# Moving attention's weighted sums one place along a hand-written interleave

## The chip, the cores and the metric

The kernel runs on one core of a Trainium2 chip. The metric is the device time of one execution in microseconds (us). A core has five engines that run side by side, each through its own queue in order: PE (TensorE, matmuls, with its weight loads shown as PEld), DVE (VectorE), ACT (ScalarE), POOL (GpSimd) and SP (SyncE, which issues most DMAs here). Results of PE land in PSUM, eight banks of 128 x 512 float32 numbers; everything else is computed from and to SBUF.

## The reference

x has 2048 rows (tokens) of 448 numbers. It is normalised, goes through an attention branch and a gated feed-forward branch, and both are added to x:

```python
xn = _layernorm(x, axis=-1)
return x + _A_ref(xn, ...) + _B_ref(xn, ...)
# _A_ref: 16 heads of 28, 4 segments of 512 tokens
for s in range(N):
    qs, ks, vs = q[:, :, s], k[:, :, s], v[:, :, s]
    logits = jnp.einsum("bhqd,bhkd->bhqk", qs, ks) * scale + mask
    p = _softmax(logits, axis=-1)
    a_dot = jnp.einsum("bhqk,bhkd->bhqd", p, vs)
    ...
    o = g * a_mem + (1.0 - g) * a_dot
# _B_ref: h = _sigmoid(xn @ w_gate) * (xn @ w_up);  h @ w_down   (448 -> 1792 -> 448)
```

`a_mem` is a read from a memory that grows from segment to segment. The change touches `a_dot` alone: the softmax's sums over the values, their division by the softmax's own sum, and the factor 1 - g.

## The kernel before, in words

**Stages.** The front part (up to line 577) normalises, makes queries, keys and values, stores them to DRAM, and computes the memory read, which goes to DRAM tensors `od`. Then, from line 785 on, three things are woven together: the feed-forward branch (`gated`, lines 166 to 270), attention within the segments (`attention`, lines 700 to 734), and at the end the output projection (`project`, lines 749 to 779). Each is a generator that stops at every `yield`. Lines 787 to 794 run through the steps of feed-forward and projection and advance attention by so many of its own steps ("places") that it gets done in proportion:

```python
want = min(round(n_att * (k - LEAD) / (N_FFN + N_OUT - LEAD - TAIL)), n_att)
```

Here `n_att` is 16 * 14 + 10 = 234 places, and the divisor is 548 + 61 - 15 - 53 = 541 steps. A feed-forward group of matmuls for gate or up (`pgu`, line 247, eleven matmuls) is followed by three steps, and a group of the down projection (`pd`, line 173, six matmuls) by two.

**Order.** `tc.manual_schedule(engines=MANUAL)` with `MANUAL = {PE, SP}` (line 55): in this stage PE and SP keep the program's order. The order on DVE, ACT and POOL is made when the kernel is built, by a scheduler that takes an instruction when its inputs should be there, the earlier in the program the sooner.

**Attention.** A `Pair` (line 583) is two heads of one segment, a `Unit` (line 670) four heads, so 32 pairs and 16 units. A pair works in ten parts:

- five parts of `scores` (603): one or two matmuls into a bank `st` of two (line 612), ACT copies the bank into the pair's buffer `w` (616, 619), POOL masks (627), DVE takes maxima (629, 633). `w` has three buffers, so pair n + 3 writes where pair n was.
- five parts of `weights` (639): the maxima are merged with POOL's help (643 to 653); DVE spreads them by a transpose to `mb` (656); then three times DVE subtracts (666) and ACT takes the exponential (667).

`Unit.finish` (681) has two parts. The first (687) has 32 small matmuls on PE, the *sums* `pa`, four keys' blocks times four heads times the values `vv`, and one DVE transpose into the buffer of the unit's second pair (690). The second is the division: a reciprocal (135), a product (136), a transpose back (693), and a store to `od` from POOL's queue that adds to what is there from the second segment on (694).

A round of 14 places per unit u goes by a table, where 0 and 1 are a score part of the unit's first and second pair, 2 is the first part of `finish` of unit u - 1, and 3 its second part:

```python
SLOT = (0, 0, 0, None, 0, 0, 2, 3, 1, 1, 1, None, 1, 1)
```

When a pair's five score parts are done, its five parts of `weights` go to a list `behind`, and each place first takes one of them. So the first pair's weights are made at places 6 to 10, and the second pair's at places 0 to 4 of the next round; the sums of a unit come at place 6 of the round after. After them SP is given the load of the next values (`load_values`, 679). Round 16 only finishes unit 15; it has a table of its own with ten places (lines 710 to 715).

Of the kernel before, what the change touches and what calls it, by code (L numbers as in the profile page):

```python
# [35 lines left out]
LEAD, TAIL = 15, 53  # L36


SLOT = (0, 0, 0, None, 0, 0, 2, 3, 1, 1, 1, None, 1, 1)

PARTS = 5

# [19 lines left out]
def kernel(  # L62
# [637 lines left out]
    def attention():  # L700
        for n in range(2):
            pairs[n].load()
        units[0].load_values()
        yield
        run, behind = {}, []
        for u in range(len(units) + 1):
            for n in range(2):
                run[n] = pairs[2 * u + n].scores() if u < len(units) else iter(())
            for k, which in enumerate(SLOT):
                if u == len(units):  # L710

                    if k > 9:
                        break
                    which = (None,) * 8 + (2, 3)
                    which = which[k]
                if behind:
                    next(behind.pop(0))
                if which is not None and which < 2 and u < len(units):
                    next(run[which])
                    n = 2 * u + which + 2  # L720
                    if which not in SLOT[k + 1:]:
                        behind += [run[which]] * PARTS
                        if n < len(pairs):
                            pairs[n].load()
                        else:
                            load_sums(n - len(pairs))
                if which == 2 and u > 0:
                    fin = units[u - 1].finish()
                    next(fin)
                    if u < len(units):  # L730
                        units[u].load_values()
                if which == 3 and u > 0:
                    next(fin)
                yield

    sums = {}
# [1 line left out]
    def load_sums(b):  # L738

        if b < 2:  # L740
            sums[b] = sb.tile([P, HG, L], F32, name="sums", tag="qk2", bufs=2)
        else:
            sums[b] = sums[b - 2]
        o3 = od[b].rearrange("(h c) n -> h c n", c=32)
        for m in range(8):
            a, c = m % 2, 4 * min(m, 6)
            nc.sync.dma_start(sums[b][64 * a:64 * a + 64, m // 2, :], o3[:, c:c + 4, :])
# [32 lines left out]

    N_OUT = 1 + NB * NT * 3 + 12
    steps = attention()
    n_att = len(units) * len(SLOT) + 10
    done = 0
    with tc.manual_schedule(engines=MANUAL):
        next(steps)
        k = sum(FILLS) + 6
# [46 lines left out]
```

## Time and profile before

| what | us |
|---|---|
| median of 3 runs (689.37 to 689.55) | 689.55 |
| the profiled execution, its own time | 689.46 |
| span of its instructions | 687.7 |
| DVE busy in the span | 567.4 |
| ACT busy in the span | 342.6 |
| POOL busy in the span | 151.3 |

The span runs from the first instruction to the end of the last; 1.8 us of the execution lie around it. In the profile's rows, a group has the line, engine, operation, tiles (output <- inputs), shapes and count, then the group's busy time, the mean length of one in ns, and after the second bar the engine's idle time just before them with what ended it. A row of the timeline has start, length, engine, line and operation, tiles and count. A row of waits has the waiting engine and line, who ended the wait, the sum in us, how often, and the longest. A row of windows has the stretch, its length, the busy time (and instructions) of PE, PEld, DVE, ACT and POOL, the granted clock of PE, the DMA engines' share and their GB/s. PE's matmuls overlap in the profile and their ends are modelled, so where PE's time goes is read from starts.

### The profile page before, as it was taken

How to read it: one execution, taken by the hardware profiler on the slowest of the kernel's cores; microseconds unless marked ns; L12 is line 12 of the kernel's file. 1: busy time of each engine (PE TensorE's matmuls, PEld its weight loads, DVE VectorE, ACT ScalarE, POOL GpSimd, SP SyncE). 2: the span in 40 equal slices, each digit the busy share in tenths (PEclk: the TensorE clock that was granted, in tenths of full speed). 3: DMA queues.
4: the chain of work that ended last, by engine and by line, in shares of the span. 5: the costliest groups of instructions: out<-in, count | busy, mean ns of one | idle time of the engine just before them, and what ended most of it. 6: DMA issues, size and time to landing. Idle time of an engine off the chain costs nothing.

```text
span 687.7 us, 10438 instructions
## 1 busy us (share of the span) xinstructions
PE 681.7 (99%) x3594; PEld 566.6 (82%) x3594; DVE 567.4 (83%) x994; ACT 342.6 (50%) x563; POOL 151.3 (22%) x349
## 2 busy tenths in 40 slices
PE   8999999999999999999999999999999999999997
PEld 7898888778878787787878878787787878878897
DVE  6765795767788988998898989989898899889863
ACT  4837555343554555543655446454653565446320
POOL 3500020101223222232332222322322322222000
PEclk9999999999999999999999999999999999999999
DMA  7446556696233323243223252314333332423342
GB/s 267 181 150 238 198 214 242 249 330 174 71 94 92 80 86 86 56 128 112 56 64 107 57 141 56 109 47 116 82 94 77 96 71 64 95 79 95 95 153 106
DMA packets 45796, 84.37 MB, mean 123 GB/s; under 512 B 6320, under 2 KB 20400, under 8 KB 45232
## 3 DMA queue, kind: packets, MB, share of 16 engines
q1 hardware_dynamic: 42736, 76.37, 35.8%
q0 software_dynamic: 3008, 7.34, 4.9%
q8 instruction: 28, 0.46, 0.3%
q14 instruction: 24, 0.20, 0.1%
HBM read 51.05 MB, written 32.64 MB: 122 GB/s over the span
## 4 chain that ended last, share of the span: by engine, by line
PE 70%; DVE 14%; issue 9%; POOL 4%; DMA 1%; ACT 1%; SPq 0%; POOLq 0%; ACTq 0%
PE pgu L247 26%; PE pd L173 13%; PE pp L355 10%; PE po L771 5%; PE pv L335 5%; PE st L612 3%; PE pa L687 3%; DVE mx L629 3%; DVE w L666 2%; POOL w L627 2%; DVE acc L174 2%; PE pmm L383 2%; PE n L401 2%; DVE hh L259 1%; DVE mx L633 1%
## 5 line engine op out<-in xcount | busy, mean ns | idle before, releaser
L247 PE MATMUL pgu<-xs,wgu 128*128 128x512 f32 x1232 | 304.1, 394 | 0.0
L247 PEld LDWEIGHTS pgu<-xs,wgu 128*128 128x128 f32 x1232 | 228.2, 188 | 47.4 <-issue 2.2
L173 PE MATMUL pd<-wdn,hh 128*128 128x448 f32 x672 | 156.0, 367 | 0.0
L627 POOL TENSOR_SCALAR_AFFINE_SELECT w<-w 128x256 f32<-128x256 f32 (+1 forms) x160 | 81.2, 509 | 236.4 <-ACT w L616 183.6
L173 PEld LDWEIGHTS pd<-wdn,hh 128*128 128x128 f32 x672 | 122.5, 188 | 12.3 <-issue 0.6
L667 ACT ACTIVATE w<-w 128x1024 f32<-128x1024 f32 (+1 forms) x96 | 87.3, 915 | 65.0 <-DVE w L666 64.2
L666 DVE TENSOR_TENSOR w<-w,mb 128x1024 f32<-128x1024 f32 (+1 forms) x96 | 98.9, 1045 | 0.1
L616 ACT ACTIVATE w<-st 128x512 f32<-128x512 f32 x128 | 74.9, 590 | 45.3 <-PE st L612 44.9
L629 DVE TRANSPOSE_TENSOR_REDUCE mx<-w 128x32 f32<-128x1024 f32 x64 | 79.0, 1235 | 17.0 <-POOL w L627 17.0
L355 PE MATMUL pp<-xs,wqk 128*128 128x512 f32 x308 | 77.7, 401 | 0.0
L174 DVE TENSOR_TENSOR acc<-pd,acc 128x448 f32<-128x448 f32 x112 | 67.1, 599 | 1.2 <-PE pd L173 1.1
L355 PEld LDWEIGHTS pp<-xs,wqk 128*128 128x128 f32 x308 | 56.8, 188 | 13.4 <-issue 2.4
L258 ACT ACTIVATE hh<-sg 128x512 fp32r<-128x512 f32 x56 | 35.2, 628 | 56.4 <-DVE sg L256 49.3
L612 PE MATMUL st<-qk 84*128 84x128 f32 (+3 forms) x256 | 61.9, 312 | 0.0
L255 ACT ACTIVATE sg<-pgu 128x512 f32<-128x512 f32 x56 | 33.2, 594 | 49.4 <-PE pgu L247 49.2
L612 PEld LDWEIGHTS st<-qk 84*128 84x128 f32 x256 | 47.6, 189 | 6.9 <-ACT w L616 0.3
L656 DVE STREAM_TRANSPOSE mb<-top 128x1024 f32<-128x1024 f32 x32 | 39.8, 1242 | 10.5 <-POOL top L653 10.1
L362 DVE TENSOR_TENSOR qk<-pp,qk 128x512 fp32r<-128x512 f32 x28 | 19.3, 688 | 29.8 <-ACT e L360 23.7
L259 DVE SCALAR_TENSOR_TENSOR hh<-sg,hh 128x512 fp32r<-128x512 f32 x56 | 38.7, 691 | 2.6 <-ACT hh L258 2.4
L335 PE MATMUL pv<-wv,xs 128*128 128x448 f32 x176 | 39.6, 376 | 0.4 <-DVE xs L102 0.3
L687 PE MATMUL pa<-w,vv 128*32 128x128 f32 (+3 forms) x512 | 39.7, 436 | 0.2
L256 DVE SCALAR_TENSOR_TENSOR sg<-sg,pgu 128x512 f32<-128x512 f32 x56 | 37.3, 665 | 1.8 <-PE pgu L247 1.6
(100 smaller groups left out, 640.6 us busy)
## 6 DMA issues: line engine op xcount, KB each, us to landing
qk<-qd SPq DMA_DIRECT2D x192, 112.0 KB
qd<-qk SPq DMA_DIRECT2D x28, 512.0 KB
raw<-in_w_ffn SPq DMA_DIRECT2D x14, 512.0 KB
vd<-vst SPq DMA_DIRECT2D x4, 1024.0 KB
vv<-vd SPq DMA_DIRECT2D x16, 256.0 KB
od<-w POOLq DMA_DIRECT2D x16, 256.0 KB, 3.8
sums<-od SPq DMA_DIRECT2D x32, 128.0 KB
out<-acc SPq DMA_DIRECT2D x16, 224.0 KB
```

The source lines that it names most:

```text
L173: T.matmul(pd[:, :D], l, r, start=n == 0, stop=n == len(mms) - 1)
L174: V.tensor_add(acc[b][:, t, :], pd[:, :D], acc[b][:, t, :])
L247: T.matmul(dst, wgu[f][:, w, side * P:(side + 1) * P], xs[b][:, a, :], start=n == 0, stop=n == len(TERMS) - 1)
L335: T.matmul(pv[:, :D], xs[b][:, a, t * P:(t + 1) * P], wv[w], start=n == 0, stop=n == len(TERMS) - 1)
L355: T.matmul(pp, wqk[c][:, w, :], xs[b][:, a, :], start=n == 0, stop=n == len(TERMS) - 1)
L612: T.matmul(st[:, at:at + L - kb * P], self.qk[:KS, 1, h, kb * P:(kb + 1) * P], self.qk[:KS, 0, h, kb * P:], start=True, stop=True)
L616: A.activation(w, st, AF.Copy)
L627: G.affine_select(d, d, pattern=pattern, base=0, channel_multiplier=-1, compare_op=ALU.is_ge, fill=MASK)
L629: V.tensor_reduce(mx[:, 16 * (n - 1):16 * (n + 1)], w3[:, n // 2, :2 * L].rearrange("p (b n) -> p b n", n=32), axis=mybir.AxisListType.X, ...
L666: V.tensor_sub(w, w, m)
L667: A.activation(w, w, AF.Exp, scale=SCALE)
L687: T.matmul(pa[32 * j:32 * j + 32, kb * P:], self.vv[:, kb, 32 * j:32 * j + 32], self.pairs[j // 2].block(j % 2, kb), start=kb == 0, stop=k ...
```

## The change

The first part of `finish` goes from place 6 to place 7, in the closing round it stays at place 8. The second part is no longer a place of the table: it goes with the place behind the first, after that place's part of `weights` and before its score part. So in a round it stands at place 8, between the first subtraction and exponential of the first pair and the first scores of the second pair. Everything else keeps its place.

```diff
-SLOT = (0, 0, 0, None, 0, 0, 2, 3, 1, 1, 1, None, 1, 1)
+SLOT = (0, 0, 0, None, 0, 0, None, 2, 1, 1, 1, None, 1, 1)
...
-        run, behind = {}, []
+        run, behind, fin = {}, [], None
...
-                    which = (None,) * 8 + (2, 3)
-                    which = which[k]
+                    which = ((None,) * 8 + (2, None))[k]
                 if behind:
                     next(behind.pop(0))
+                if fin:
+                    next(fin)
+                    fin = None
                 if which is not None and which < 2 and u < len(units):
...
                 if which == 2 and u > 0:
                     fin = units[u - 1].finish()
                     next(fin)
                     if u < len(units):
                         units[u].load_values()
-                if which == 3 and u > 0:
-                    next(fin)
                 yield
```

## The prediction, as it was put on record

> **What bounds the kernel now.** I read the page's busy times and its dearest groups first, then the busy time by stage, and then the list of waits for the few places where PE stops.
>
> ```profile
> span 687.7 us, 10438 instructions
> PE 681.7 (99%) x3594; PEld 566.6 (82%) x3594; DVE 567.4 (83%) x994; ACT 342.6 (50%) x563; POOL 151.3 (22%) x349
> L247 PE MATMUL pgu<-xs,wgu 128*128 128x512 f32 x1232 | 304.1, 394 | 0.0
> L247 PEld LDWEIGHTS pgu<-xs,wgu 128*128 128x128 f32 x1232 | 228.2, 188 | 47.4 <-issue 2.2
> 203.12:643.00 439.88, 439.67 (x2372) 359.77 (x2375) 397.00 (x647) 230.39 (x362) 116.91 (x280) 1.00 0.33 85
> PEld pa L687 <- issue: 17.9, 68, 0.4
> PEld pa L687 <- ACT w L667: 2.1, 4, 0.8
> PEld pa L687 <- POOL w L627: 0.7, 2, 0.4
> ```
>
> The fifth row is the stretch from attention's first sums to its last: its length, then busy time of PE, PEld, DVE, ACT and POOL. PE has no hole in it, and the granted clock is 1.00. A busy PE can hide waits, since ends are modelled, so I look at the spacing instead. A pgu matmul is shown as 394 ns long, but its weight load takes 188 ns and 39 ns of idle stand before each (47.4 us over 1232): one matmul every 227 ns, eleven in 2.5 us. Only 2.2 us of that idle has a name; the rest is the load waiting its turn. So PE runs back to back, and a wait that goes is time that goes.
>
> In this stretch the waits list charges PE one thing that I can name, the sums (pa, L687) waiting for exponentials: 2.1 us in 4 waits. To check it I compare two undisturbed groups with the three that are longer (start and length, then what follows):
>
> ```profile
> 203.12 2.36 PE L687 MATMUL pa<-w,vv 128*32 128x512 f32 x32
> 205.41 1.47 PE L173 MATMUL pd<-wdn,hh 128*128 128x448 f32 x6
> ```
>
> ```profile
> 318.62 2.36 PE L687 MATMUL pa<-w,vv 128*32 128x512 f32 x32
> 320.91 2.79 PE L247 MATMUL pgu<-xs,wgu 128*128 128x512 f32 x11
> ```
>
> ```profile
> 289.05 3.33 PE L687 MATMUL pa<-w,vv 128*32 128x512 f32 x32
> 292.31 1.48 PE L173 MATMUL pd<-wdn,hh 128*128 128x448 f32 x6
> 293.63 2.65 PE L247 MATMUL pgu<-xs,wgu 128*128 128x512 f32 x11
> ```
>
> ```profile
> 435.95 3.26 PE L687 MATMUL pa<-w,vv 128*32 128x512 f32 x32
> 439.14 2.81 PE L247 MATMUL pgu<-xs,wgu 128*128 128x512 f32 x11
> 441.79 1.37 PE L173 MATMUL pd<-wdn,hh 128*128 128x448 f32 x6
> ```
>
> ```profile
> 495.62 2.60 PE L687 MATMUL pa<-w,vv 128*32 128x512 f32 x32
> 498.15 2.79 PE L247 MATMUL pgu<-xs,wgu 128*128 128x512 f32 x11
> 500.77 1.37 PE L173 MATMUL pd<-wdn,hh 128*128 128x448 f32 x6
> ```
>
> An undisturbed group takes 205.41 - 203.12 = 320.91 - 318.62 = 2.29 us to the next start, in front of a pd and of a pgu alike. The others take 3.26, 3.19 and 2.53 us: 0.97 + 0.90 + 0.24 = 2.11 us too much, the 2.1 us of the waits list. The "issue" idle (17.9 us) and POOL's 0.7 us lie inside undisturbed groups too, whose length they don't change, so they are not to be gained.
>
> **The change part by part.** No instruction is added or removed. Rounds 1 to 16 hold one unit's sums each. The closing round 16 has a table of its own, with the sums at place 8 and the rest at place 9 both before and after, so fifteen rounds differ.
>
> (1) *PE: the 32 sums go from place 6 to place 7.* PE's order is the program's. Attention advances 234 places over 541 steps of the other work, 2.16 per five steps. Five steps are one pgu group (2.5 us, three steps behind it) and one pd group (1.2 us, two steps). Followed through lines 781 to 794, this puts between places 6 and 7 no matmuls in rounds 1 and 3, a pd and a pgu in round 2, a pd in rounds 4, 6, 8, 10, 12 and 14, and a pgu in rounds 5, 7, 9, 11, 13 and 15. The three long groups are those of rounds 4, 9 and 11. They get later by 293.63 - 292.31 = 1.32 us, 441.79 - 439.14 = 2.65 us and 500.77 - 498.15 = 2.62 us. The waits were 0.97, 0.90 and 0.24 us, so all three are covered if the exponentials keep their dates:
>
> ```profile
> 290.89 0.16 PEld L687 LDWEIGHTS pa<-w,vv 128*32 128x32 f32 x8 [0.83 <-ACT w L667]
> 289.26 1.58 ACT L667 ACTIVATE w<-w 128x1024 f32<-128x1024 f32 x2 [0.15 <-DVE w L666]
> 437.05 0.62 ACT L667 ACTIVATE w<-w 128x512 f32<-128x512 f32 x1
> 496.05 0.62 ACT L667 ACTIVATE w<-w 128x512 f32<-128x512 f32 x1
> ```
>
> In round 4 the last exponential ends at 290.84 and the sums would start at 289.05 + 1.32 = 290.37. The load that waited for it was ready 0.83 us before 290.89, at 290.06, 1.0 us into the group; that becomes 291.4, with 0.5 us to spare. In rounds 9 and 11 the last exponential ends at 437.67 and 496.67, before the sums' new starts at 438.60 and 498.24. Gain: 2.11 us. What follows the sums changes from pd to pgu or back, which costs nothing, by the two undisturbed groups. The scores (L612) stay at places 5 and 8, on either side, with the same matmuls between; what lies between places 6 and 7 comes 2.29 us earlier.
>
> (2) *DVE: four instructions per round move.* This is what they cost, in round 3 (start, length):
>
> ```profile
> 266.02 0.67 DVE L690 STREAM_TRANSPOSE w<-pa 128x512 f32<-128x512 f32 x1
> 266.62 1.21 DVE L666 TENSOR_TENSOR w<-w,mb 128x1024 f32<-128x1024 f32 x1
> 267.75 0.24 DVE L135 RECIPROCAL rc<-w 128x16 f32<-128x16 f32 x1
> 267.91 0.55 DVE L174 TENSOR_TENSOR acc<-pd,acc 128x448 f32<-128x448 f32 x1
> 268.39 0.67 DVE L136 SCALAR_TENSOR_TENSOR w<-w,gate_n,rc 128x448 f32<-128x448 f32 x1
> 268.98 1.22 DVE L666 TENSOR_TENSOR w<-w,mb 128x1024 f32<-128x1024 f32 x1
> 270.11 0.70 DVE L693 STREAM_TRANSPOSE w<-w 128x512 f32<-128x512 f32 x1
> ```
>
> Together 0.67 + 0.24 + 0.67 + 0.70 = 2.28 us. In program order the transpose of the sums now follows the maxima's transpose instead of preceding it, and the other three follow the first subtraction. But DVE's and ACT's order is not written down: only PE and SP keep the program's, and the rows show the two already woven (subtraction, reciprocal, product, subtraction). So the diff does not tell DVE's new order. Its total is unchanged. Per round it is 397.00 / 15 = 26.5 us of 439.88 / 15 = 29.3 us: 2.8 us free. PE waits for none of the four. What they can delay is a subtraction, through it an exponential on ACT, and behind that the copy of a score bank (L616), which PE does wait for. I bound this from both sides. From below: the first subtraction no longer has three of the four ahead of it, which could save more than nothing, but I count no gain, since the three waits are all that PE shows. From above: all 2.28 us in front of a copy, against the margin that it has:
>
> ```profile
> 210.01 0.59 ACT L616 ACTIVATE w<-st 128x512 f32<-128x512 f32 x1
> 210.97 0.40 PE L612 MATMUL st<-qk 84*128 84x512 f32 x1
> 271.25 0.58 ACT L616 ACTIVATE w<-st 128x512 f32<-128x512 f32 x1
> 273.48 0.40 PE L612 MATMUL st<-qk 84*128 84x384 f32 x2
> ```
>
> The first copy ends at 210.60 and its bank is written again at 210.97, a margin of 0.37 us; the second ends at 271.83 for 273.48, 1.65 us. All 2.28 us would cost PE 1.91 and 0.63 us, 1.27 us in the mean of the two, 19 us in 15 rounds. I take nothing, by the second row: there a subtraction waited behind two of the four, its exponential held the copy, and PE still did not wait. Both ends stay for the range.
>
> (3) *The store and SP's load.* The store of the shares (L694) leaves POOL's queue one place later, ahead of the masks (L627) that are queued there; the load of the next values (L679) waits for the sums on SP.
>
> ```profile
> 212.04 0.56 POOL L694 DMA_DIRECT2D od<-w  x1 [1.01 <-DVE w L693]
> DMA to landing us min/median/max: 2.3/3.8/5.1
> 219.64 0.60 ACT L616 ACTIVATE w<-st 128x512 f32<-128x512 f32 x1 [0.54 <-PE st L612]
> 205.54 0.54 SPq L679 DMA_DIRECT2D vv<-vd  x1
> ```
>
> The store's buffer is written next by the copy at 219.64. A landing after 3.8 us, at 215.8, leaves 3.8 us, and one place is 1.3 to 2.65 us: covered by the rest of the round. The values are wanted a round (29 us) after their load at 205.54. Both cost nothing. If the store came two places late, it would eat its margin and hold that copy, which is the road of (2) again.
>
> Sum: -2.11 us. The profiled execution took 689.46 us (687.7 of span and 1.8 around it), 0.09 under the median of the runs, 689.55. 689.46 - 2.11 = 687.35; by the median 687.44. I say **687.4 us**.
>
> **The rivals.**
>
> *A. DVE is the real bound (689.5 us).* PE would leave the sums sooner and meet a score copy that waits for DVE. For it: 397.0 of 439.88 us is 90%, the highest share of any engine whose ends are measured. Against it: 2.8 us a round are free, and PE stops nowhere but at the sums. The Trainium skill ("Perfetto Trace Analysis", section Identifying the Most-Contended Engine) would have TensorE's nearness to its limit read from the weight loads' share, not from matmul's. By that rule PE stands at 82% and DVE leads, and the change gives nothing; this trace disagrees as far as its 227 ns go, because each 188 ns load waits 39 ns for the running matmul.
>
> *B. Part given back (688.5 us).* The new weave costs some copies a few tenths. Three stalls at the 0.37 us of the tight margin cost 1.1 us: 687.4 + 1.1 = 688.5.
>
> *C. The divisions get into the subtractions' way (691.6 us), slower.* The place is the second and third subtraction of a round's first pair, the price the 0.91 us of reciprocal and product put in front of the exponential that holds a copy. Against a margin like round 1's it is 0.91 - 0.37 = 0.54 us. If half the rounds are as tight (7.5), 4.1 us: 687.4 + 4.1 = 691.5. It cancels the gain from a delay of 2.11 / 7.5 + 0.37 = 0.65 us. For it: round 1's margin is less than one of the moved transposes (0.67 us). Against: round 3, above.
>
> *D. The change does not do what it says (689.5 us).* The exponentials of rounds 4, 9 and 11 come later by as much as the sums. DVE's freedom of 2.8 us a round speaks against.
>
> **How the numbers follow.** The forecast has 0.50, A 0.08, B 0.12, C 0.25, D 0.05. About 0.2% (1.4 us) is what a measurement of this kernel can tell from no change. The forecast is faster by 0.3%. B lies 0.9 us under the old time, so it counts as the same, with A and D: 0.25. C counts as slower: 0.25. A little of the forecast's chance is at its edge, so I give faster 0.49, same 0.25, slower 0.26. The range starts at 686.9 (half a microsecond under the forecast, for the small waits at scores that might go too) and ends at 691.6, the time of C; half of C, the dearer half up to the 19 us of (2), is left out above. The forecast's own range is 686.9 to 688.1.
>
> **What would show it.** Right: in rounds 4, 9 and 11 the sums take 2.29 us, the wait of L687 for L667 is gone from the list, and PE's scores show no new wait. C would show as PE idle before L612 charged to ACT's L616, with L135 and L136 between subtractions. D would show as groups of over 2.3 us at the new place. The prediction is wrong if L616 holds PE for over 0.7 us in sum, or if DVE's order changes far from the moved places.

## The result, and the profile after

| | us |
|---|---|
| before, median of 8 runs | 689.53 |
| changed, median of 8 runs | 687.44 |
| ratio, with its 95% interval | 0.9969 (0.9958 to 0.998) |
| profiled execution of the changed kernel; its span | 687.43; 685.7 |

The kernel is faster by 2.1 us, 0.3%. One execution of the eight took 1377.36 us and the other seven 687.23 to 687.49; it is not part of the ratio.

The page of the changed kernel, its row for the middle stretch (from the first sums to the last, columns as before), and PE's rows in the list of waits at the sums and at the scores:

```profile
span 685.7 us, 10450 instructions
PE 679.6 (99%) x3594; PEld 565.5 (82%) x3594; DVE 566.7 (83%) x994; ACT 341.6 (50%) x563; POOL 147.6 (22%) x349
L247 PE MATMUL pgu<-xs,wgu 128*128 128x512 f32 x1232 | 303.6, 393 | 0.0
L247 PEld LDWEIGHTS pgu<-xs,wgu 128*128 128x128 f32 x1232 | 228.2, 188 | 46.9 <-issue 2.4
203.18:640.42 437.24, 437.16 (x2369) 358.31 (x2368) 395.31 (x645) 228.39 (x360) 113.04 (x280) 1.00 0.34 85
PEld pa L687 <- issue: 19.1, 73, 0.4
PEld pa L687 <- POOL w L627: 1.3, 4, 0.4
PEld st L612 <- ACT w L616: 0.7, 3, 0.3
```

The stretch went from 439.88 to 437.24 us. The row "pa L687 <- ACT w L667" of 2.1 us is gone from the list. The busy shares are the same as before: PE 99%, PEld 82%, DVE 83%. Shares don't show a change of this size, only the waits and the spacing of starts do.

The chain that ended last, first before and then changed, shows the same thing in another way:

```profile
PE 70%; DVE 14%; issue 9%; POOL 4%; DMA 1%; ACT 1%; SPq 0%; POOLq 0%; ACTq 0%
```

```profile
PE 97%; DMA 1%; DVE 1%; SPq 0%; issue 0%; ACT 0%; ACTq 0%
```

The chain is followed back from releaser to releaser. Before, at the wait of round 9's sums (437.7 us), it left PE and ran back to 249.6 us through the work of DVE, ACT and POOL, 188 us without a piece of PE's; a third of that is "issue", time for which the profile names no wait. Without those waits it stays on PE.

PE's sums and what follows in rounds 4, 9 and 11, where before had 3.26, 3.19 and 2.53 us, and then in the closing round:

```profile
290.29 2.36 PE L687 MATMUL pa<-w,vv 128*32 128x512 f32 x32
292.58 2.79 PE L247 MATMUL pgu<-xs,wgu 128*128 128x512 f32 x11
```

```profile
437.44 2.36 PE L687 MATMUL pa<-w,vv 128*32 128x512 f32 x32
439.73 1.48 PE L173 MATMUL pd<-wdn,hh 128*128 128x448 f32 x6
```

```profile
496.12 2.36 PE L687 MATMUL pa<-w,vv 128*32 128x512 f32 x32
498.41 1.48 PE L173 MATMUL pd<-wdn,hh 128*128 128x448 f32 x6
```

```profile
640.42 2.50 PE L687 MATMUL pa<-w,vv 128*32 128x512 f32 x32
642.85 1.48 PE L771 MATMUL po<-wo,xs 128*128 128x448 f32 x6
```

All three are 2.29 us to the next start. The closing round's sums, which didn't move, are 2.43 us: a new wait of 0.14 us.

Summed over PE's spacing from the first sums to the end, the time behind the sums' matmuls fell by 1.96 us, behind pgu by 0.31 and behind pd by 0.10, and behind the scores it rose by 0.27: together 2.10 us.

### The profile page after: what moved, and what is told of

The parts are those of the page before. It is cut to its first block, busy times and chain, and to the rows that moved or that the text cites. A ratio compares the mean times of both kernels' runs of the same rounds, so it can differ in the third digit from the quotient of the medians.

```text
span 685.7 us, 10450 instructions
## 1 busy us (share of the span) xinstructions
PE 679.6 (99%) x3594; PEld 565.5 (82%) x3594; DVE 566.7 (83%) x994; ACT 341.6 (50%) x563; POOL 147.6 (22%) x349
## 4 chain that ended last, share of the span: by engine, by line
PE 97%; DMA 1%; DVE 1%; SPq 0%; issue 0%; ACT 0%; ACTq 0%
PE pgu L247 41%; PE pd L173 20%; PE pp L355 10%; PE st L612 6%; PE pa L687 5%; PE po L771 5%; PE pv L335 5%; PE pmm L383 2%; PE n L401 2%; DMA acc<-in_x 1%; PE pt L95 1%; PE pk L375 1%; DMA vv<-vd 0%; DVE stats L294 0%; DVE acc L775 0%
## 5 line engine op out<-in xcount | busy, mean ns | idle before, releaser
L667 ACT ACTIVATE w<-w 128x1024 f32<-128x1024 f32 (+1 forms) x96 | 87.4, 916 | 88.4 <-DVE w L666 87.9
L666 DVE TENSOR_TENSOR w<-w,mb 128x1024 f32<-128x1024 f32 (+1 forms) x96 | 98.6, 1035 | 0.2
L174 DVE TENSOR_TENSOR acc<-pd,acc 128x448 f32<-128x448 f32 x112 | 67.2, 600 | 1.1 <-PE pd L173 1.1
L687 PE MATMUL pa<-w,vv 128*32 128x128 f32 (+3 forms) x512 | 37.9, 436 | 0.0
```

The source lines that it names most:

```text
L174: V.tensor_add(acc[b][:, t, :], pd[:, :D], acc[b][:, t, :])
L666: V.tensor_sub(w, w, m)
L667: A.activation(w, w, AF.Exp, scale=SCALE)
L687: T.matmul(pa[32 * j:32 * j + 32, kb * P:], self.vv[:, kb, 32 * j:32 * j + 32], self.pairs[j // 2].block(j % 2, kb), start=kb == 0, stop=k ...
```

## The experiments

The theory is that of the prediction: PE gains its waits for exponentials in rounds 4, 9 and 11, and nothing else. Rival 1 is that DVE gains, because the division no longer stands ahead of the subtractions. Rival 2 is that PE gains a little in every moved round.

Most runs are the kernel before, with its loop written so that the two places can be chosen for each round. The closing round keeps 8 and 9.

```diff
-SLOT = (0, 0, 0, None, 0, 0, 2, 3, 1, 1, 1, None, 1, 1)
+SLOT = (0, 0, 0, None, 0, 0, None, None, 1, 1, 1, None, 1, 1)
+sums_at, division_at = lambda u: 6, lambda u: 7        # the values differ by run
...
                 if behind:
                     next(behind.pop(0))
+                if fin and k == (9 if u == len(units) else division_at(u)):
+                    next(fin)
+                    fin = None
...
+                if u > 0 and k == (8 if u == len(units) else sums_at(u)):
+                    fin = units[u - 1].finish()
+                    next(fin)
+                    if u < len(units):
+                        units[u].load_values()
+                if fin and k == (9 if u == len(units) else division_at(u)):
+                    next(fin)
+                    fin = None
...
```

**One half of the change at a time.** First the division alone:

```diff
+sums_at, division_at = lambda u: 6, lambda u: 8
```

> The sums stay at place 6 in every round; only the division and the store go to place 8. Theory (PE's waits for exponentials in rounds 4, 9 and 11 are all that was gained): those waits stay, 689.5 us, within 0.5 us. Rival 1 (the division's later place lets the subtractions go first on DVE, and that is the gain): 687.4 us. Rival 2 (PE gains a little in each moved round from what stands beside the sums, about 2.1 / 15 = 0.14 us a round): 689.5 us, since no sums move.

Measured: 689.41 us, ratio 0.9999 (0.999 to 1.0007). PE's starts show the waits still there, 0.97, 0.79 and 0.21 us. Rival 1 falls.

Then the sums alone. The division stays at place 7, where it now follows the sums by the last three lines of the loop above:

```diff
+sums_at, division_at = lambda u: 7, lambda u: 7
```

> The sums go to place 7 in every round, the division and the store stay at place 7, right behind them. Theory: 687.4 us, and the waits of the sums for exponentials are gone. Rival 1 (the division's place is the gain): 689.5 us. Rival 2 (a little in each round): 687.4 us.

Measured: 687.30 us, ratio 0.9968 (0.9956 to 0.9981). The sums' move alone makes the whole gain.

**Three rounds, and the other twelve.**

```diff
+sums_at, division_at = lambda u: 7 if u in (4, 9, 11) else 6, lambda u: 8 if u in (4, 9, 11) else 7
```

> Sums at place 7 and division at place 8 in rounds 4, 9 and 11 alone, the other twelve as before. Theory: nearly the whole gain, 687.4 us, within 0.5 us. Rival 2 (0.14 us in each moved round): 3 x 0.14 = 0.4 us, 689.1 us. Rival 1 (the division's place): a fifth of the gain too, 689.1 us.

Measured: 688.17 us, ratio 0.9981 (0.9973 to 0.999). That is 1.3 of the 2.1 us, outside the bounds of the theory as it was put, and far from Rival 2's 0.4. The three waits are gone, but another round waits. PE in round 5 of this run, then ACT's last exponential of that round's pair in this run and in the kernel before:

```profile
317.62 3.29 PE L687 MATMUL pa<-w,vv 128*32 128x512 f32 x32
320.83 0.50 PE L247 MATMUL pgu<-xs,wgu 128*128 128x512 f32 x1
```

```profile
318.73 0.63 ACT L667 ACTIVATE w<-w 128x512 f32<-128x512 f32 x1
```

```profile
318.70 0.63 ACT L667 ACTIVATE w<-w 128x512 f32<-128x512 f32 x1
```

From the first start to the next group's the sums take 320.83 - 317.62 = 3.21 us: 0.92 us of wait (0.93 before rounding). The exponential ends at 319.36 in this run and at 319.33 before, so it kept its date. The sums start at 317.62, where before had 318.62. PE came a microsecond sooner because it had not waited in round 4, and met the same exponential in front of it. A wait of one round covers the next.

The opposite choice:

```diff
+sums_at, division_at = lambda u: 6 if u in (4, 9, 11) else 7, lambda u: 7 if u in (4, 9, 11) else 8
```

> The opposite: sums at place 6 and division at place 7 in rounds 4, 9 and 11, in the other twelve at places 7 and 8. Theory: the three waits stay about as long as they were (0.97, 0.90 and 0.24 us, if DVE's order in those rounds keeps the exponentials' dates), 689.5 us; up to 1 us less if the moves in other rounds bring the exponentials forward. Rivals 1 and 2: 12 of 15 parts of the gain, 687.8 us.

Measured: 689.80 us, ratio 1.0006 (0.9997 to 1.0015). Twelve moved rounds bring nothing. The waits, from PE's starts, are 0.99, 1.11 and 0.40 us, and 0.12 in the closing round: 2.61 us, 0.5 more than before. Rival 2 falls with this run and the last, at the size that it was given.

**Round 5 too.**

```diff
+sums_at, division_at = lambda u: 7 if u in (4, 5, 9, 11) else 6, lambda u: 8 if u in (4, 5, 9, 11) else 7
```

> As the run with rounds 4, 9 and 11 one place later, and round 5 too. There round 5 waited 0.93 us for an exponential, in place of the wait of round 4 that was taken away. Theory (a wait of one round covers the next, since the exponentials keep their dates when PE comes sooner): this wait goes as well, round 6 may get up to 0.3 us: 687.4 to 687.7 us. Rival (the moved division in round 4 made round 5's exponentials late, so now round 6's get late in the same way): about 688.2 us again, with a wait of some 0.9 us in round 6.

Measured: 687.06 us, ratio 0.9965 (0.9952 to 0.9977). No group of sums is longer than 2.29 us, in round 6 neither. So the wait in round 5 of the run before came from PE's earlier arrival, not from DVE's new order.

**The same waits, made shorter in another way.** Here nothing moves between places. The block of keys that needs the last exponential comes later within the sums:

```diff
-            for kb in range(NT):
+            for kb in (0, 2, 1, 3):
```

> The kernel before, with all places as they were; inside the sums the blocks of keys go 0, 2, 1, 3 instead of 0, 1, 2, 3, so that the block that needs a pair's last exponential comes 0.43 us later in the group. DVE's, ACT's and POOL's order stay the same. Theory: round 4 waits 0.56 us instead of 0.97 (now for the middle exponential), round 9 0.47 instead of 0.90, round 11 nothing instead of 0.24: 1.1 us gained, 688.4 us. A rival by which the sums' neighbours or the division's place on DVE made the gain: 689.5 us, since neither changes.

Measured: 688.46 us, ratio 0.9985 (0.9976 to 0.9994), the forecast of the theory to a tenth. DVE, ACT and POOL have the same instructions in the same order as before. PE's rows in rounds 4, 9 and 11:

```profile
289.11 2.92 PE L687 MATMUL pa<-w,vv 128*32 128x512 f32 x32
291.96 0.47 PE L173 MATMUL pd<-wdn,hh 128*128 128x448 f32 x1
```

```profile
435.64 2.88 PE L687 MATMUL pa<-w,vv 128*32 128x512 f32 x32
438.46 0.50 PE L247 MATMUL pgu<-xs,wgu 128*128 128x512 f32 x1
```

```profile
494.94 2.36 PE L687 MATMUL pa<-w,vv 128*32 128x512 f32 x32
497.23 0.50 PE L247 MATMUL pgu<-xs,wgu 128*128 128x512 f32 x1
```

2.85, 2.82 and 2.29 us: waits of 0.56, 0.53 and 0.00 us, where 0.56, 0.47 and 0 were expected.

**One place further, in either direction.** One place earlier:

```diff
+sums_at, division_at = lambda u: 5, lambda u: 7
```

> Sums at place 5 (behind that place's scores) in every round, one place earlier than before; the division stays at place 7. Theory: more rounds wait for exponentials. If the exponentials' dates don't move when PE waits (what one round waits, the next needn't), the waits of the rounds, worked out from the dates of before and the matmuls between places 5 and 6, sum up to 3.6 us, 2.1 + 1.5: 691.0 us. If the exponentials move along with PE, each round pays for itself, 15.8 us in all: 703 us. A rival by which the waits have nothing to do with the sums' place: 689.5 us.

Measured: 701.39 us, ratio 1.0172 (1.0159 to 1.0186). From PE's starts, 14 of the sums' 16 groups are more than 0.1 us too long, by 14.2 us in all, near the 15.8 us of "each round pays for itself". One of them, round 10, and DVE's rows for PE in the list of waits:

```profile
469.86 1.70 PE L687 MATMUL pa<-w,vv 128*32 128x512 f32 x12
472.40 1.49 PE L687 MATMUL pa<-w,vv 128*32 128x384 f32 x20 [0.84 <-ACT w L667]
473.82 1.42 PE L247 MATMUL pgu<-xs,wgu 128*128 128x512 f32 x5
```

```profile
DVE sg L256 <- PE pgu L247: 6.1, 6, 1.8
DVE acc L174 <- PE pd L173: 5.8, 10, 1.2
```

These two are waits of DVE for PE; before, they were 1.6 and 1.1 us. When PE waits in nearly every round, DVE runs out of work and waits for PE in turn, so the exponentials get later along with PE and a wait covers less of the next. That reading fits the rows; how much of the 14.2 us comes by it was not measured by itself.

One place later (the sums ahead of that place's scores, as the second pair's buffer is free only behind them):

```diff
+sums_at, division_at = lambda u: 8, lambda u: 9
```

> Sums at place 8 (before that place's scores) and division at place 9 in every round, one place later than in the changed kernel. Theory (only the waits for exponentials were to be gained, and they are gone at place 7 but for 0.14 us in the closing round, which doesn't move): the same as the changed kernel, 687.4 us, within 0.4 us. A rival by which each place later brings its own 2 us: 685.3 us. The other side: the divisions now meet the second pair's scores and the store comes later, and a score copy holds PE: 688.5 us or more.

Measured: 688.26 us, ratio 0.9984 (0.9975 to 0.9993), 0.8 us over the changed kernel. No group of sums waits here, nor in the closing round. Others do; two rows of its list of waits:

```profile
ACT w L616 <- DMA od<-w: 5.8, 3, 2.5
PEld st L612 <- ACT w L616: 1.3, 3, 0.5
```

ACT's copy of scores waits for the store to leave its buffer, a wait that neither the kernel before nor the changed one has, and PE waits longer for the copies. The execution in this trace is the fastest of the eleven (687.71 to 689.36 us), 0.3 us over that of the changed kernel. So it shows where PE now waits, but not all of the 0.8 us.

**Is there a faster one?** The changed kernel, the same with the other block order, and the four rounds, side by side on one chip:

```diff
-            for kb in range(NT):
+            for kb in (0, 2, 1, 3):      # in the changed kernel
```

> The changed kernel with the blocks of keys in the sums taken 0, 2, 1, 3. DVE's, ACT's and POOL's order stay those of the changed kernel. Theory: the last wait for an exponential, 0.14 us in the closing round, goes: 687.3 us, 0.1 under the changed kernel. If the block order had a gain of its own (besides the waits), its 1.0 us of the kernel before would come again: 686.4 us.

> The changed kernel itself, beside the next run on the same chip: 687.4 us.

> The kernel with only rounds 4, 5, 9 and 11 one place later, beside the changed kernel on the same chip: 687.1 us, 0.3 us under it, since it has no wait of the sums at all (the changed one 0.14 us in the closing round) and DVE's order of before nearly everywhere, with fewer small waits at the scores. If its lead came from the chip of its first runs: 687.4 us.

Measured: 687.22 us (687.07 to 687.34) with the other block order, 687.30 (687.15 to 687.89) for the changed kernel and 687.05 (687.04 to 687.11) for the four rounds, ratios 0.9967, 0.997 and 0.9965 to the kernel before, with overlapping intervals. The closing round's wait goes with the block order, as the first fence shows, but its 0.14 us is no more than the spread of the runs. The second fence has the four rounds' waits:

```profile
640.38 2.36 PE L687 MATMUL pa<-w,vv 128*32 128x512 f32 x32
642.67 1.07 PE L771 MATMUL po<-wo,xs 128*128 128x448 f32 x4
```

```profile
PEld pa L687 <- ACT w L667: 0.3, 1, 0.3
PEld st L612 <- ACT w L616: 0.3, 1, 0.3
```

The four rounds were lowest in both of their sessions, and their waits at the scores are those of before (0.3 us) where the changed kernel has 0.7. Here each of their executions (up to 687.11) lies under each of the changed kernel's (from 687.15). The lead of 0.25 us is small, though, and the ratios' intervals don't separate the two.

## Why the prediction was right, point by point

**The forecast.** 687.4 us was forecast, 687.44 measured. That it agrees to a tenth is in part luck: the sums gave 1.96 us instead of 2.11, the scores took 0.27, and 0.41 came from spacing that the prediction didn't count.

**PE's bound.** Shown: three ways of shortening the same waits (all rounds, four rounds, another block order) gave 2.1, 2.4 and 1.0 us where the waits fell by 1.96, 2.10 and 1.02 us, and lengthening them by 12.1 us cost 11.9. Rival A, DVE as the real bound, falls. By the rule named beside it (the Trainium skill, "Perfetto Trace Analysis", Identifying the Most-Contended Engine) the weight loads' 82% would have left room; the share was 82% with the waits and without them, and each microsecond of wait still counted. That section names the share of peak FLOPs beside the weight loads', and this was not worked out here.

**Step (1), the sums.** Right in mechanism and size, 2.11 us forecast for rounds 4, 9 and 11, and all of it gone. The exponentials there, changed kernel:

```profile
289.32 1.58 ACT L667 ACTIVATE w<-w 128x1024 f32<-128x1024 f32 x2 [0.15 <-DVE w L666]
```

```profile
436.54 0.62 ACT L667 ACTIVATE w<-w 128x512 f32<-128x512 f32 x1
```

```profile
494.00 0.62 ACT L667 ACTIVATE w<-w 128x512 f32<-128x512 f32 x1
```

In round 4 the last one ends at 290.90, 0.61 us into the sums; the weights were said to be wanted 1.0 us in. The other two end before the sums start. No exponential came later along with the sums, so rival D falls.

What the step didn't see is that the rounds are coupled. It took each wait by itself. With only those three rounds moved, PE met round 5's exponentials, and the gain was 1.3 us. It was whole because round 5 moved as well, which the step had not asked for: in that it was lucky.

The closing round, called unchanged, paid 0.14 us for another reason. With the four rounds moved, PE came to it at 640.30 us, sooner than the 640.42 of the changed kernel, and did not wait. What differs is DVE's order ahead of the round's last exponential. DVE in the kernel before and in the changed one:

```profile
637.92 0.58 DVE L174 TENSOR_TENSOR acc<-pd,acc 128x448 f32<-128x448 f32 x1
638.43 2.34 DVE L666 TENSOR_TENSOR w<-w,mb 128x1024 f32<-128x1024 f32 x2
```

```profile
636.29 1.23 DVE L666 TENSOR_TENSOR w<-w,mb 128x1024 f32<-128x1024 f32 x1
637.44 0.62 DVE L174 TENSOR_TENSOR acc<-pd,acc 128x448 f32<-128x448 f32 x1
637.97 1.21 DVE L666 TENSOR_TENSOR w<-w,mb 128x1024 f32<-128x1024 f32 x1
```

An addition of the down projection's result (L174) now stands between the two subtractions (L666), and the last exponential ends 0.95 us into the sums (641.37 less 640.42), where it was 0.37 us before and 0.40 with the four rounds, whose DVE keeps the order of before here. The run of the other twelve rounds has the changed order here too, and it waits 0.12 us although PE comes to it no sooner than before (642.70 against 642.59 us).

**Step (2), DVE.** The cost taken, nothing, was nearly right. DVE's new order in round 3 of the changed kernel, where the sums themselves stayed among the same matmuls:

```profile
266.10 0.67 DVE L690 STREAM_TRANSPOSE w<-pa 128x512 f32<-128x512 f32 x1
266.70 1.18 DVE L666 TENSOR_TENSOR w<-w,mb 128x1024 f32<-128x1024 f32 x1
...
268.34 0.24 DVE L135 RECIPROCAL rc<-w 128x16 f32<-128x16 f32 x1
268.50 1.16 DVE L666 TENSOR_TENSOR w<-w,mb 128x1024 f32<-128x1024 f32 x1
269.57 0.67 DVE L136 SCALAR_TENSOR_TENSOR w<-w,gate_n,rc 128x448 f32<-128x448 f32 x1
...
270.76 0.70 DVE L693 STREAM_TRANSPOSE w<-w 128x512 f32<-128x512 f32 x1
```

The second subtraction starts at 268.50, where it was 268.98: the product now stands behind it. Rival C needed the opposite. Waits at the scores went from 0.3 to 0.7 us, the direction of rival B, at a third of its 1.1 us. Rival C had asked for margins like round 1's 0.37 us in half the rounds. Followed through the trace of the kernel before, only five of its score copies end less than 0.5 us before their bank is written again.

Two of the prediction's signs did not hold as they were put. The scores do show new waits (three instead of one), and at 0.7 us they stand at the limit that it had set for being wrong. And DVE's order changed in the closing round too, more than 10 us behind the last moved division, whose store is issued at 622.79 us. The time came right all the same, so a new order was no sign of a new time; in the run with the division alone DVE's order changed in several rounds, and nothing was gained or lost.

**Step (3), the store.** No cost, but the cover that it counted on was thinner than said. It expected at least 1.15 us to be left (3.8 less 2.65). The tightest store of the changed kernel, and the copy that writes its buffer next:

```profile
565.84 0.86 POOL L694 DMA_DIRECT2D od<-w  x1
```

```profile
570.21 0.59 ACT L616 ACTIVATE w<-st 128x512 f32<-128x512 f32 x1
```

```profile
DMA to landing us min/median/max: 2.3/3.9/5.1
```

With the median landing that is 570.21 - 565.84 - 3.9 = 0.47 us. The same two rows in the kernel before:

```profile
562.51 0.87 POOL L694 DMA_DIRECT2D od<-w  x1 [2.77 <-DVE w L693]
```

```profile
572.55 0.59 ACT L616 ACTIVATE w<-st 128x512 f32<-128x512 f32 x1
```

From issue to copy there were 10.04 us, and 4.37 are left. The step had counted one place as what PE does in it, 1.3 to 2.65 us. This store came 3.33 us later and the copy 2.34 sooner. The first round, from which the margin was read, hardly changed: its store and copy are 7.6 us apart in both kernels. There the store also lands faster than the median that was used: the first four stores, which don't add to what is there, take 2.3 us, and all later ones 3.7 us or more. One place later the cover is gone, as the run with places 8 and 9 shows.

**What stays open.** The spacing behind pgu and pd matmuls, where nothing was changed, also fell by 0.41 us in sum. It falls by 0.34 to 0.41 us in each run that moves the sums in twelve or fifteen rounds to place 7, and by 0.10 at most in those that move three or four. So a small part of rival 2 is left, some 0.03 us a round, but the scores take 0.20 to 0.31 us back in the same runs. No run here tells why the spacing fell.

## What to carry to other kernels

On an engine without gaps, look for the groups that are longer than their like, find which input was late in them, and move the consumer only as far as that input's date asks; here one place was worth 2.1 us, a place further lost 0.8 and a place in the other direction 11.9. Check the neighbours' margins together with the waits, since a wait that goes brings the engine sooner to the next meeting. And where a store frees a buffer, take its margin from every round and not from one: here one fell from 10.0 to 4.4 us between issue and next write while another stayed at 7.6, and a place further the stores were the limit. A step that looks untouched, as the closing round, can change too when the order on other engines is made anew.

## What the runs showed that was not expected

An exponential's date did not follow PE when PE came a microsecond sooner (319.36 against 319.33 us), but did follow when PE waited in nearly every round (14.2 us of waits, near the 15.8 worked out for rounds that pay for themselves). In the first case DVE ran the same rows at the same times as before from 305.9 us on, within 0.04 us, and the chain of the kernel before has no piece of PE's there; in the second DVE waited for PE. In the closing round the last exponential followed PE even without such waits (with four rounds moved both came 2.3 us sooner), so it depends on the stretch.
